# Reordering the quarter products of a seven-product FFN output and moving an epsilon from GpSimd to ScalarE (top-k attention and SwiGLU)

## The chip, the cores and the metric

The kernel runs on one core of one Trainium2 chip. The metric is the device time of one execution in microseconds (us); lower is better. The names of the engines in the profile are: PE is TensorE's matmuls, PEld its weight loads, DVE is VectorE, ACT is ScalarE, POOL is GpSimd, SP is SyncE, which here only issues transfers.

## The reference: what is computed

Attention over 8 batches and 8 heads with 576 positions of 64 elements, in which each query keeps only its 32 largest scores, and then a SwiGLU block on the 4608 rows of 512 that come out. All is float32.

```python
# attention: q, k, v of shape (8, 8, 576, 64)
scores = scale * np.matmul(q, k.transpose(0, 1, 3, 2))
kth = np.partition(scores, -top_k, axis=-1)[..., -top_k:-top_k + 1]   # top_k = 32
scores = np.where(scores >= kth, scores, -1000000000.0)
scores = scores - np.max(scores, axis=-1, keepdims=True)
attn = np.exp(scores)
attn = attn / (np.sum(attn, axis=-1, keepdims=True) + 1e-09)
x = np.matmul(attn, v)                      # brought to (4608, 512)
# FFN: w_gate, w_val of (512, 1536), w_out of (1536, 512)
g = x @ w_gate
silu = g * (1.0 / (1.0 + np.exp(-g)))
out = silu * (x @ w_val) @ w_out
```

## The kernel before

**Units.** The attention is cut into 160 units: one batch, one tile of 128 queries (the fifth tile of a batch has 64) and one pair of heads. In one pass of the main loop several units are in work at once, each at another step. VectorE picks the 32 largest scores of unit n, GpSimd and ScalarE form the exponentials of unit n-1, VectorE and ScalarE normalize unit n-2, TensorE transposes unit n-3 and multiplies unit n-4 with v. The order of instructions on every engine is fixed when the program is built: each engine takes its own in the order in which the code emits them.

**FFN.** As soon as 256 rows of the attention's result are there (`done`), their FFN can be computed: a block. There are 18 blocks, and `feed` is a generator that gives a block's matmuls in pieces. The main loop puts such pieces among the steps of the attention, as many as a credit allows.

**The epsilon, before.** `weigh` takes exp with the row sum as an accumulated output. A unit later, `normalize` first adds the epsilon on GpSimd, then takes the reciprocal on VectorE and scales on ScalarE:

```python
def penalize(n):
    ...
    nc.gpsimd.tensor_scalar_mul(bias[:, 0:nh], m[:, 0:nh, 0], -scale)
    nc.gpsimd.tensor_tensor(e[:, every], e[:, every], sc[:, every], ALU.add)      # L338

def weigh(n):
    ...
    for t, hs in enumerate(heads):
        nc.scalar.activation(                                                     # L347
            e[:, hs], e[:, hs], AF.Exp, bias=bias[:, t : t + 1], scale=scale,
            accum_out=tot[:, t : t + 1],
        )
    st["tot"] = tot

def normalize(n):
    ...
    nc.gpsimd.tensor_scalar_add(tot[:, 0:nh], tot[:, 0:nh], EPS)                  # L357
    yield
    nc.vector.reciprocal(tot[:, 0:nh], tot[:, 0:nh])                              # L359
    yield
    for t, hs in enumerate(heads):
        nc.scalar.mul(e[:, hs], e[:, hs], tot[:, t : t + 1])                      # L362
```

**The main loop**, cut to the order in which one pass emits its steps:

```python
flush(on_act)              # ScalarE work that the FFN pieces left for later
next(norm, None)           # GpSimd: epsilon of unit n-2
penalize(n - 1)            # GpSimd: bias, e + sc
flush(on_pool)             # GpSimd work that was left for later
run(turn(n - TURN))        # TensorE: transposes of e (L374), ScalarE: copies (L375)
finish_unit(n - VALUES)    # TensorE: e times v (L403)
next(nxt, None)            # TensorE: scores of unit n+1 (L281, L295)
weigh(n - 1)               # ScalarE: exp
run(nxt)                   # ScalarE: copies of these scores to sc (L286, L300)
dve(2, beside=False)       # VectorE: top-k steps of unit n
...
pieces(2)                  # FFN pieces on TensorE
flush(on_act)
flush(on_pool)
dve(1)
dve(1)
next(norm, None)           # VectorE: reciprocal
run(norm)                  # ScalarE: scaling
...                        # more top-k steps and up to 7 more pieces
```

**The seven products.** For the last matrix product of a block (all blocks but the first) the kernel uses a scheme with seven products in place of eight. The 256 rows are halved into early and late, the 1536 inner elements into two halves, the 512 outputs into two halves. P1 to P7 are called quarters here: six matmuls each (twelve records in the profile[...]) into one PSUM area. Their operands are sums and differences that GpSimd forms in place in `hs`, in `s32` (which takes the place of `xT`) and in the weights:

```python
def quarter(i, ps):
    for m in range(MQ):                       # MQ = 6
        s, r = m // 2, m % 2
        lhsT = {
            1: lambda: hs[s][:, r, early],
            2: lambda: hs[s + MS // 2][:, r, early],
            3: lambda: hs[s][:, r, late],
            4: lambda: hs[s + MS // 2][:, r, late],
            5: lambda: hs[s][:, r, late],
            6: lambda: s32[:, m],
            7: lambda: s32[:, m],
        }[i]()
        nc.tensor.matmul(ps, lhsT, T[i][m], start=m == 0, stop=m == MQ - 1)      # L543
        if m % 3 == 2:
            yield 0.75
...
# order: P1, P7, P5, P6, then
    def keep_y():
        nc.scalar.copy(b[:], y_ps[:])                                             # L577
        def sum_up():                         # tt is a GpSimd addition, L529
            tt(b[:, 1], b[:, 0], b[:, 1])
            tt(o[:, 1, DH:], o[:, 1, DH:], b[:, 1])
            tt(a[:], a[:], b[:, 1:2].to_broadcast([P, 2, DH]))
        on_pool.append(sum_up)

    yield from quarter(6, y_ps[:, 1])
    on_act.append(keep_y)
    flush(on_act)
    flush(on_pool)
    for s in range(MS // 2):                                                      # L591
        nc.gpsimd.tensor_tensor(
            hs[s][:, :, late],
            hs[s + MS // 2][:, :, early],
            s32[:, 2 * s : 2 * s + 2],
            ALU.subtract,
        )
    x_ps2 = ps_f.tile([P, 2, DH], FP32, tag="f", name="x_ps")
    yield from quarter(4, x_ps2[:, 1])
    yield from quarter(3, x_ps2[:, 0])
    ...
    def rest_x():
        nc.scalar.copy(middle, x_ps2[:])                                          # L605
        on_pool.append(lambda: tt(middle, middle, a[:]))
    on_act.append(rest_x)
    y_ps2 = ps_f.tile([P, DH], FP32, tag="f", name="y_ps")
    yield from quarter(2, y_ps2[:])
    def rest_y():
        nc.scalar.copy(o[:, 0, 0:DH], y_ps2[:])                                   # L613
        def stores():
            tt(o[:, 0, 0:DH], o[:, 0, 0:DH], b[:, 0])
            for t in range(2):
                store(o[:, t, :], kb * BLK + t * P)
        on_pool.append(stores)
    on_act.append(rest_y)
```

The pool `ps_f` has three PSUM buffers, which the FFN's tiles take in turn. `on_act` and `on_pool` are lists of work for ScalarE and GpSimd that is emitted at the next flush.

Of the kernel before, what the change touches and what calls it, by code (L numbers as in the profile page):

```python
# [8 lines left out]
AF = mybir.ActivationFunctionType  # L9
ALU = mybir.AluOpType  # L10
FP32 = mybir.dt.float32
# [4 lines left out]
P = 128  # L16
# [3 lines left out]
EPS = 1.0e-9  # L20
# [7 lines left out]
def kernel(  # L28
# [37 lines left out]
    nc = tc.nc  # L66
# [14 lines left out]
    consts = ctx.enter_context(tc.tile_pool(name="consts", bufs=1))  # L81
# [7 lines left out]
    ps_f = ctx.enter_context(tc.tile_pool(name="ps_f", bufs=3, space=PSUM))  # L89
# [5 lines left out]
    for i in range(NV):  # L95
        vt = consts.tile([P, P], FP32, name=f"vlast{i}")
        nc.vector.memset(vt[:], 0.0)
        vlast.append(vt)
    wg = consts.tile([P, KC, DFF], FP32, name="wg")
    wv = consts.tile([P, KC, DFF], FP32, name="wv")  # L100
    wo = consts.tile([P, MC, DM], FP32, name="wo")
# [86 lines left out]
    def rounding(n):  # L188
        for _ in range(n):
            next(weight, None)  # L190
# [70 lines left out]
    def n_heads(qt):  # L261

        return 1 if qt == J else 2
# [39 lines left out]
    def select(n):  # L303

        nh = n_heads(units[n][1])
        sc = state[n]["sc"]
        m = small.tile([P, 2, TOP_K], FP32, tag="m", name="m", bufs=2)
        heads = [slice(t * S, (t + 1) * S) for t in range(nh)]
        rest = work.tile([P, 2 * S], FP32, tag="rest", name="rest", bufs=1)
        e = work.tile([P, 2 * S], FP32, tag="e", name="e", bufs=4)  # L310
        state[n] |= dict(m=m, e=e, heads=heads)
        cur = sc
        rounds = TOP_K // 8
        for r in range(rounds):
            for t, hs in enumerate(heads):
                nc.vector.max(m[:, t, 8 * r : 8 * r + 8], cur[:, hs])  # L316
                yield
            if r < rounds - 1:
                for t, hs in enumerate(heads):
                    nc.vector.match_replace(  # L320
                        rest[:, hs], m[:, t, 8 * r : 8 * r + 8], cur[:, hs], LOWEST
                    )
                    yield
                cur = rest
        for t, hs in enumerate(heads):
            nc.vector.tensor_scalar(  # L326
                e[:, hs], sc[:, hs], m[:, t, TOP_K - 1 : TOP_K], FAR, ALU.is_lt, ALU.mult
            )
# [12 lines left out]
    def weigh(n):  # L341

        st = state[n]
        e, heads, bias = st["e"], st["heads"], st.pop("bias")
        tot = small.tile([P, 2], FP32, tag="tot", name="tot")
        for t, hs in enumerate(heads):
            nc.scalar.activation(  # L347
                e[:, hs], e[:, hs], AF.Exp, bias=bias[:, t : t + 1], scale=scale,
                accum_out=tot[:, t : t + 1],
            )  # L350
        st["tot"] = tot

    def normalize(n):
        st = state[n]
        tot, e, heads = st.pop("tot"), st["e"], st.pop("heads")
        nh = len(heads)
        nc.gpsimd.tensor_scalar_add(tot[:, 0:nh], tot[:, 0:nh], EPS)  # L357
        yield
        nc.vector.reciprocal(tot[:, 0:nh], tot[:, 0:nh])  # L359
        yield  # L360
        for t, hs in enumerate(heads):
            nc.scalar.mul(e[:, hs], e[:, hs], tot[:, t : t + 1])  # L362
# [62 lines left out]
    def store(o, g0):  # L425

        at = g0
        while at < g0 + P:
            b, c = divmod(at, S)
            j, p0 = divmod(c, P)  # L430
            n = min(g0 + P - at, S - c, P - p0)
            r0 = b * S + (c if j == J else J * p0 + j)
            dst = out[r0 : r0 + n, :] if j == J else out[r0 : r0 + J * (n - 1) + 1 : J, :]
            nc.sync.dma_start(dst, o[at - g0 : at - g0 + n, :])
            at += n

    on_act, on_pool = [], []

    def flush(queue):
        while queue:  # L440
            queue.pop(0)()

    def feed(kb):
# [50 lines left out]
        o = ffn.tile([P, 2, DM], FP32, tag="o", name="o", bufs=1)  # L494
# [29 lines left out]
        DH = DM // 2  # L524
        y_ps = ps_f.tile([P, 2, DH], FP32, tag="f", name="y_ps")
        x_ps = ps_f.tile([P, 2, DH], FP32, tag="f", name="x_ps")

        def tt(out, in0, in1):
            nc.gpsimd.tensor_tensor(out, in0, in1, ALU.add)  # L529

        def quarter(i, ps):
            for m in range(MQ):
# [10 lines that stand above are left out]
                nc.tensor.matmul(  # L543
                    ps, lhsT, T[i][m], start=m == 0, stop=m == MQ - 1
                )
                if m % 3 == 2:
                    yield 0.75
# [19 lines left out]
        a = ffn.tile([P, 2, DH], FP32, tag="gv", name="p57", bufs=3)  # L567
# [6 lines left out]
        b = ffn.tile([P, 2, DH], FP32, tag="gv", name="p16", bufs=3)  # L574
# [15 lines left out]
# [4 lines that stand above are left out]
                s32[:, 2 * s : 2 * s + 2],  # L594
                ALU.subtract,
            )
        x_ps2 = ps_f.tile([P, 2, DH], FP32, tag="f", name="x_ps")
        yield from quarter(4, x_ps2[:, 1])
        yield from quarter(3, x_ps2[:, 0])
        middle = o[:].rearrange("p t d -> p (t d)")[:, DH : 3 * DH].rearrange(  # L600
            "p (t d) -> p t d", t=2
        )

        def rest_x():
            nc.scalar.copy(middle, x_ps2[:])  # L605
            on_pool.append(lambda: tt(middle, middle, a[:]))

        on_act.append(rest_x)
        y_ps2 = ps_f.tile([P, DH], FP32, tag="f", name="y_ps")
        yield from quarter(2, y_ps2[:])  # L610

        def rest_y():
            nc.scalar.copy(o[:, 0, 0:DH], y_ps2[:])  # L613

            def stores():
                tt(o[:, 0, 0:DH], o[:, 0, 0:DH], b[:, 0])
                for t in range(2):
                    store(o[:, t, :], kb * BLK + t * P)

            on_pool.append(stores)  # L620

        on_act.append(rest_y)

    NU = len(units)
    todo = list(range(NBLK))
# [21 lines left out]
    def fetch(n):  # L647

        b, qt, hp = units[n]
        i = b * NHP + hp  # L650
        if qt == 0:
            yield from prep(i)
        if qt == J and i + NHP < len(pairs):
            load(i + NHP)

    def pieces(n):
        for _ in range(n):
            if credit[0] >= 1:
                credit[0] -= piece()

    def run(steps):
        for _ in steps:
            pass
# [18 lines left out]
    for n in range(NU + VALUES):  # L682
        nh = n_heads(units[n][1]) if n < NU else 1
        topk = select(n) if n < NU else no
        over[n - 1] = normalize(n - 1) if 0 <= n - 1 < NU else no
        nxt = scores(n + 1) if n + 1 < NU else no
        ahead = fetch(n + 2) if n + 2 < NU else no
        norm = over.pop(n - 2, no)

        def dve(k, beside=True):  # L690

            for _ in range(k * nh):
                next(topk, None)
                due[0] += 5 / 11 if beside else 0
                if due[0] >= 1:
                    due[0] -= 1
                    rounding(1)

        if n >= NU - NHP:
            credit[0] = 8.0  # L700
        else:
            credit[0] = min(credit[0] + (4.45 if nh == 2 else 2.25), 8.0)
        flush(on_act)
        next(norm, None)
        if 0 <= n - 1 < NU:
            penalize(n - 1)
        flush(on_pool)
        if 0 <= n - TURN < NU:
            run(turn(n - TURN))
        if n >= VALUES:  # L710
            finish_unit(n - VALUES)
        next(nxt, None)
        if 0 <= n - 1 < NU:
            weigh(n - 1)
        run(nxt)

        dve(2, beside=False)
        if 2 <= n + 2 < NHP:
            load(n + 2)
        if n < NHP:  # L720
            load_v(n)
        pieces(2)
# [4 lines that stand above are left out]
        next(norm, None)  # L727
        run(norm)
        next(ahead, None)
        pieces(1)  # L730
        next(ahead, None)
        dve(1)
        pieces(1)
        dve(2)
        run(topk)
        pieces(6)
# [50 lines left out]
```

## Time and profile before

| | |
|---|---|
| time, median of 3 runs (lowest to highest) | 1920.52 us (1919.66 to 1921.52) |
| span of the profiled execution | 1918.4 us |
| TensorE matmul busy | 1727.4 us, 90% |
| VectorE busy | 1621.0 us, 84% |
| ScalarE busy | 1170.2 us, 61% |
| GpSimd busy | 1062.6 us, 55% |
| mean granted TensorE clock | 0.952 of full speed |

A profile is read here in this way. The busy table gives one sum for each engine over the whole execution. The slices cut the execution into 40 equal parts, with one digit each for the busy tenths. The waits tell, for an instruction's line and the engine that it runs on, which instruction ended the idle time ahead of it: the total in us, how often, and the longest. In the timeline, each row is an instruction, or several of one kind that follow each other, with its start, its length and, in brackets, the idle time before it and what ended it. Lines such as L591 are lines of the kernel before. An engine's idle time costs something only where that engine, at that moment, sets how fast the rest can go on.

### The profile page before, as it was taken

The numbers are of one execution on the slowest core, as the hardware profiler recorded it, in microseconds if no ns is written. First come the engines' busy times: TensorE is split into PE (matmuls) and PEld (weight loads), VectorE is DVE, ScalarE is ACT, GpSimd is POOL, SyncE is SP. The second block draws the span as 40 slices with busy tenths as digits, with TensorE's granted clock in tenths as the row PEclk, the third lists the DMA queues.
The fourth block names the chain that finished last, engine by engine and source line by source line (L and its number), as shares of the span: only waits on it lengthen the run. The fifth ranks groups of instructions, "written<-read, shape, count | busy, mean of one in ns | idle before, by whom it ended". The sixth has DMA issues, their size and how long they took to land.

```text
span 1918.4 us, 30988 instructions
## 1 busy us (share of the span) xinstructions
PE 1727.4 (90%) x10756; PEld 1418.9 (74%) x10756; DVE 1621.0 (84%) x3476; ACT 1170.2 (61%) x2855; POOL 1062.6 (55%) x1167
## 2 busy tenths in 40 slices
PE   3437789989999999898999999989999999899988
PEld 2336558778888778786778877878788878787877
DVE  7999889998899979897889989988898979998300
ACT  5656666666666566566656666656675657565432
POOL 4556655645565646464455655645556645556534
PEclk7668899989999999899999999999999999999989
DMA  7322212000300011000210003000210002000000
GB/s 186 87 80 79 66 31 59 12 1 2 81 7 12 1 46 44 12 1 13 54 35 1 12 10 80 1 12 1 64 26 12 1 14 51 12 1 12 1 12 11
DMA packets 111261, 59.68 MB, mean 31 GB/s; under 512 B 89088, under 2 KB 97280, under 8 KB 111104
## 3 DMA queue, kind: packets, MB, share of 16 engines
q1 hardware_dynamic: 109904, 57.41, 11.3%
q8 instruction: 85, 1.39, 0.3%
q14 instruction: 72, 0.59, 0.1%
q10 hardware_dynamic: 1200, 0.30, 0.1%
HBM read 48.23 MB, written 9.44 MB: 30 GB/s over the span
## 4 chain that ended last, share of the span: by engine, by line
PE 70%; POOL 10%; DVE 8%; ACT 7%; issue 4%; DMA 0%; SPq 0%; POOLq 0%; ACTq 0%; DVEq 0%
PE f L457 35%; PE av L403 7%; PE etps L374 7%; PE x_ps L543 7%; PE s L295 5%; PE y_ps L543 4%; DVE m L316 4%; POOL e L338 4%; DVE rest L320 3%; ACT e L347 2%; ACT sc L300 2%; PE s L281 2%; POOL p L529 1%; PE av L394 1%; POOL size L124 1%
## 5 line engine op out<-in xcount | busy, mean ns | idle before, releaser
L316 DVE MAX8 m<-rest 128x8 f32<-128x576 f32 x864 | 614.5, 745 | 2.2
L320 DVE MATCH_REPLACE8 rest<-m,rest 128x576 f32<-128x576 f32 x576 | 423.6, 741 | 0.0
L457 PE MATMUL f<-xT,wg 128*128 128x256 f32 x1728 | 405.6, 385 | 0.0
L457 PE MATMUL f<-xT,wv 128*128 128x256 f32 x1728 | 397.9, 381 | 0.0
L338 POOL TENSOR_TENSOR e<-e,sc 128x1152 f32<-128x1152 f32 (+1 forms) x160 | 382.9, 2393 | 27.0 <-DVE e L326 26.8
L457 PEld LDWEIGHTS f<-xT,wg 128*128 128x128 f32 x1728 | 324.9, 191 | 66.7 <-issue 23.7
L457 PEld LDWEIGHTS f<-xT,wv 128*128 128x128 f32 x1728 | 324.3, 190 | 55.6 <-issue 13.5
L485 POOL TENSOR_TENSOR h<-h,half_g 128x512 f32<-128x512 f32 x108 | 138.4, 1282 | 366.2 <-ACT h L484 363.0
L374 PE MATMUL etps<-ident,e 128*128 128x128 f32 (+1 forms) x1312 | 191.2, 291 | 130.3 <-POOL size L114 46.8
L347 ACT ACTIVATE e<-e,bias 128x576 f32<-128x576 f32 x288 | 222.0, 776 | 125.6 <-POOL e L338 125.3
L374 PEld LDWEIGHTS etps<-ident,e 128*128 128x128 f32 (+1 forms) x1312 | 161.8, 149 | 162.7 <-POOL size L114 50.1
L375 ACT COPY et<-etps 128x512 f32<-128x512 f32 (+1 forms) x448 | 185.0, 483 | 144.6 <-PE etps L374 143.0
L316 DVE MAX8 m<-sc 128x8 f32<-128x576 f32 x288 | 205.2, 748 | 75.7 <-ACT sc L300 46.9
L490 POOL TENSOR_TENSOR h<-h,val 128x512 f32<-128x512 f32 x108 | 140.2, 1298 | 158.3 <-ACT val L489 158.2
L362 ACT ACTIVATE e<-e,tot 128x576 f32<-128x576 f32 x288 | 210.7, 782 | 5.4 <-DVE tot L359 5.1
L320 DVE MATCH_REPLACE8 rest<-m,sc 128x576 f32<-128x576 f32 x288 | 211.6, 741 | 0.0
L295 PE MATMUL s<-kqT 64*128 64x288 f32 x1024 | 173.0, 446 | 8.9 <-ACT kqT L255 6.0
L403 PE MATMUL av<-et,v 128*64 128x128 f32 (+1 forms) x2560 | 174.6, 282 | 0.0
L300 ACT COPY sc<-s 128x288 f32<-128x288 f32 x512 | 164.7, 408 | 2.5 <-PE s L295 2.5
L482 ACT ACTIVATE h<-f 128x512 f32<-128x512 f32 x108 | 64.8, 600 | 164.0 <-PE f L457 163.5
L326 DVE TENSOR_SCALAR e<-sc,m 128x576 f32<-128x576 f32 x288 | 159.0, 589 | 3.8 <-DVE m L316 0.5
L403 PEld LDWEIGHTS av<-et,v 128*64 128x64 f32 x2560 | 137.6, 146 | 23.4 <-issue 7.3
(70 smaller groups left out, 2035.0 us busy)
## 6 DMA issues: line engine op xcount, KB each, us to landing
kq_in<-in_k_dram SPq DMA_DIRECT2D x64, 128.0 KB, 2.8
v<-in_v_dram SPq DMA_DIRECT2D x32, 256.0 KB, 3.2
kq_in<-in_q_dram SPq DMA_DIRECT2D x62, 128.0 KB, 3.0
w<-in_moe_w_gate_dram SPq DMA_DIRECT2D x24, 256.0 KB, 2.7
w<-in_moe_w_val_dram SPq DMA_DIRECT2D x24, 256.0 KB, 2.7
w<-in_moe_w_out_dram SPq DMA_DIRECT2D x24, 256.0 KB, 2.6
out_dram<-o SPq DMA_DIRECT2D x40, 128.0 KB, 2.4
out_dram<-o SPq DMA_DIRECT2D x16, 256.0 KB, 2.4
```

The costliest lines, as they stand in the source:

```text
L295: nc.tensor.matmul(ps[:, 0:half], slab[d, q0 : q0 + P], slab[d, k0 : k0 + half])
L300: nc.scalar.copy(sc[:, i * half : (i + 1) * half], ps[:, 0:half])
L316: nc.vector.max(m[:, t, 8 * r : 8 * r + 8], cur[:, hs])
L320: nc.vector.match_replace(rest[:, hs], m[:, t, 8 * r : 8 * r + 8], cur[:, hs], LOWEST)
L338: nc.gpsimd.tensor_tensor(e[:, every], e[:, every], sc[:, every], ALU.add)
L347: nc.scalar.activation(e[:, hs], e[:, hs], AF.Exp, bias=bias[:, t : t + 1], scale=scale, accum_out=tot[:, t : t + 1],)
L362: nc.scalar.mul(e[:, hs], e[:, hs], tot[:, t : t + 1])
L374: nc.tensor.transpose(ps[0:kl, c * P : (c + 1) * P], e[:, k0 : k0 + kl], ident[:])
L375: nc.scalar.copy(et[0:kl, c0 : c0 + cn, :], ps[0:kl, 0 : cn * P].rearrange("p (c j) -> p c j", c=cn),)
L403: nc.tensor.matmul(av[hh * R : (hh + 1) * R, 0:ql], v_last[:, hh, :] if c == J else vt[:, hh, c, :], moving, start=last and c == 0, stop=c ...
L457: nc.tensor.matmul(ps[:, i, :], w[:, kc, m * P : (m + 1) * P], x[:, kc, :], start=(kc == 0), stop=(kc == KC - 1),)
L543: nc.tensor.matmul(ps, lhsT, T[i][m], start=m == 0, stop=m == MQ - 1)
```

## The change

Two things are changed.

- Of the last three quarters of a block, P2 now comes first and P4 and P3 follow. Before it was P4, P3, P2. P3 reads what the subtraction behind P6 (L591) writes, and P2 doesn't; the order is meant to give GpSimd more time for it. The copies and additions of the results change places accordingly: the quarter area of P2 is finished first, and the addition of the middle half of the output now stands ahead of the stores.
- The epsilon is added to the row sums by ScalarE, as an Identity activation with the epsilon as its bias, right behind exp. GpSimd no longer does it a unit later, so the reciprocal on VectorE doesn't depend on GpSimd's queue any more.

```diff
+    eps = consts.tile([P, 1], FP32, name="eps")
+    nc.vector.memset(eps[:], EPS)
...
                 accum_out=tot[:, t : t + 1],
             )
+        nh = len(heads)
+        nc.scalar.activation(tot[:, 0:nh], tot[:, 0:nh], AF.Identity, bias=eps[:])
         st["tot"] = tot

     def normalize(n):
...
-        nc.gpsimd.tensor_scalar_add(tot[:, 0:nh], tot[:, 0:nh], EPS)
-        yield
         nc.vector.reciprocal(tot[:, 0:nh], tot[:, 0:nh])
...
+        y_ps2 = ps_f.tile([P, DH], FP32, tag="f", name="y_ps")
+        yield from quarter(2, y_ps2[:])
+
+        def rest_y():
+            nc.scalar.copy(o[:, 0, 0:DH], y_ps2[:])
+            on_pool.append(lambda: tt(o[:, 0, 0:DH], o[:, 0, 0:DH], b[:, 0]))
+
+        on_act.append(rest_y)
         x_ps2 = ps_f.tile([P, 2, DH], FP32, tag="f", name="x_ps")
         yield from quarter(4, x_ps2[:, 1])
         yield from quarter(3, x_ps2[:, 0])
...
         def rest_x():
             nc.scalar.copy(middle, x_ps2[:])
-            on_pool.append(lambda: tt(middle, middle, a[:]))
-
-        on_act.append(rest_x)
-        y_ps2 = ps_f.tile([P, DH], FP32, tag="f", name="y_ps")
-        yield from quarter(2, y_ps2[:])
-
-        def rest_y():
-            nc.scalar.copy(o[:, 0, 0:DH], y_ps2[:])

             def stores():
-                tt(o[:, 0, 0:DH], o[:, 0, 0:DH], b[:, 0])
+                tt(middle, middle, a[:])
                 for t in range(2):
                     store(o[:, t, :], kb * BLK + t * P)

             on_pool.append(stores)

-        on_act.append(rest_y)
+        on_act.append(rest_x)
...
         flush(on_act)
-        next(norm, None)
         if 0 <= n - 1 < NU:
             penalize(n - 1)
```

## The prediction

> **What bounds the kernel now.** I read the page first: the busy table and the slices.
>
> ```profile
> PE 1727.4 (90%) x10756; PEld 1418.9 (74%) x10756; DVE 1621.0 (84%) x3476; ACT 1170.2 (61%) x2855; POOL 1062.6 (55%) x1167
> ...
> PE   3437789989999999898999999989999999899988
> ...
> PEclk7668899989999999899999999999999999999989
> ```
>
> TensorE is busiest, VectorE follows, and the granted clock is below full speed mainly in the first slices. An average over different stages says little, so I asked for three stages (columns: stage, length, busy time of PE, PEld, DVE, ACT, POOL, then clock, DMA share, GB/s):
>
> ```profile
> 0.00:340.00 340.00, 223.10 (x1255) 169.80 (x1256) 301.85 (x689) 208.55 (x532) 197.76 (x260) 0.80 0.30 83
> 340.00:1850.00 1510.00, 1442.52 (x9228) 1195.76 (x9227) 1319.15 (x2788) 946.35 (x2295) 836.05 (x878) 0.98 0.08 20
> 1850.00:1919.00 69.00, 61.82 (x276) 53.38 (x275) 0.00 (x0) 15.27 (x28) 28.77 (x30) 0.97 0.04 8
> ```
>
> Up to about 340 us VectorE and the chain around it set the pace (302 of 340 us). After that TensorE does (1443 of 1510, then 62 of 69), so what is left to win there is its idle time, about 1579 - 1504 = 75 us. The waits of TensorE from 340 us to the end name it (total us, times, longest):
>
> ```profile
> PE x_ps L543 <- POOL h L591: 29.7, 13, 3.2
> PE etps L374 <- issue: 27.0, 15, 3.8
> PE etps L374 <- ACT e L362: 11.7, 9, 4.1
> ```
>
> The largest is P3 waiting for the difference that GpSimd writes into `hs` at L591. The other two are transposes that wait for the scaled `e`, at places where little FFN work is left to fill TensorE. One instance of the first, from the timeline (start, length, engine, line, operation, idle before it):
>
> ```profile
> 762.76 2.75 PE L543 MATMUL x_ps<-t,h 128*128 128x256 f32 x12
> ...
> 764.09 0.60 ACT L577 COPY p<-y_ps 128x512 f32<-128x512 f32 x1
> 764.77 0.73 POOL L529 TENSOR_TENSOR p<-p 128x256 f32<-128x256 f32 x1 [1.04 <-ACT p L577]
> ...
> 765.58 0.72 POOL L529 TENSOR_TENSOR o<-o,p 128x256 f32<-128x256 f32 x1
> 766.26 1.27 POOL L529 TENSOR_TENSOR p<-p,p 128x512 f32<-128x512 f32 x1
> ...
> 767.49 2.11 POOL L591 TENSOR_TENSOR h<-h,xT 128x256 f32<-128x256 f32 x3
> ...
> 768.27 4.54 PE L543 MATMUL x_ps<-wo,h 128*128 128x256 f32 x12 [2.75 <-POOL h L591]
> ```
>
> `x_ps<-t,h` is P4; its next twelve, `x_ps<-wo,h`, are P3. Behind P6, ScalarE copies its sums (L577), GpSimd makes three additions of results (L529) and only then the operands for P3 (L591). P4 covers part of that, 2.6 us; then TensorE stands for 2.75 us. P2 needs nothing of it (it reads the early columns of `hs`), yet comes after P3.
>
> The epsilon shows in two views: the waits of VectorE from 340 to 1850 us, and the instructions that touch `tot`.
>
> ```profile
> DVE tot L359 <- POOL tot L357: 104.0, 41, 12.5
> DVE m L316 <- ACT sc L300: 41.1, 34, 4.9
> ```
>
> ```profile
> L357 POOL TENSOR_SCALAR tot<-tot x160: 214/219/892, 39.5 to 1841.0; 128x2 f32<-128x2 f32 x128, 128x1 f32<-128x1 f32 x32
> ```
>
> VectorE loses 104 us to an operation of 0.22 us that stands in GpSimd's queue behind the FFN products. But nearly all of it falls where TensorE is the bound, so it is mostly slack of an engine that isn't the limit.
>
> [...] exp, tanh, absolute values and scalings alternate all through, with one ACT_TABLE_LOAD (1.28 us) at the very start. [...] after the waits at 765, 977 and 1257 us P3 took 4.54, 4.54 and 4.45 us instead of 2.75 to 2.86, after the ten others it did not.
>
> **The change, part by part.**
>
> (a) *P2 first.* Same quarter products, same number; by the instruction order P2 takes P4's place, P4 that of P3 and P3 that of P2, and the attention work between them stays where it is. So P3's operands get the length of one more quarter, 2.6 us. Thirteen waits sum to 29.7 us; five are longer than 2.6 (2.75, 3.18, 3.07, 2.75, 3.19) and leave together 1.9. Saving: 27.8 us, on TensorE's own path.
>
> (b) *Clock.* Without those gaps the three slow P3 come back to 2.8: 3 x 1.7 = 5 us saved.
>
> (c) *Given back.* Where the FFN runs dry after a block, VectorE becomes the bound. A saving passes through only as far as VectorE was itself idle there. At 768 the saving is 2.75 + 1.7, VectorE's idle time ahead of the dry stretch is 0.34 + 2.89; at 1647 it is 2.75 against 0.32 + 1.20. About 1.2 each: 2.4 us lost.
>
> (d) *Epsilon.* GpSimd loses 160 x 0.22 us; with its start, 0.30 us from one operation to the next (780.12 to 780.42 in the timeline), ahead of the `bias` and `e` + `sc` operations. ScalarE gains 160 Identities behind exp and ahead of the copies of the scores. Each must wait until the accumulator readout behind exp (median 188 ns) has ended; up to now the next copy overlapped it. [...] Where the chain runs GpSimd, exp, scores, VectorE, a unit pays +0.4 - 0.3 = 0.1. That is the early stage: 20 of the 160 units start their addition before 290 us, so +2 us. In the TensorE-bound units it is hidden on both sides. About six block ends go dry (381, 779, 883, 1270, 1656, 1760 us); there the Identity delays the scores by 0.4, and the last copy of the block is now the larger one (L605, 0.59 us, instead of L613, about 0.4): 6 x 0.6 = 3.6 us. In the last units one addition of 0.7 us leaves GpSimd's chain. Sum: +4.9 us.
>
> (e) *End.* After the last quarter the copy is 0.59 instead of 0.37 us and the addition 1.27 instead of 0.72: +0.8 us.
>
> (f) *VectorE's reciprocal* no longer waits. Its 104 us become waits for `sc` from ScalarE, which TensorE releases: zero for the end.
>
> Sum: -27.8 - 5 + 2.4 + 4.9 + 0.8 = -24.7 us, so 1920.5 - 24.7 = 1896 us.
>
> **Rivals.**
>
> *VectorE was the real limit, and the epsilon wait is what matters.* For it: 104 us of waits, 84% busy, units of about 9 us in dry stretches against 10.5 in full ones. Against it: in full stretches the matmuls follow each other without a gap for 10.5 us a unit, and the longest reciprocal waits (8.9, 10.0, 12.6 us near 1800) lie where TensorE has no gap at all. If true, 50 us or more would go: below 1870.
>
> *ScalarE's added step sits on the path.* For it: exp and the score copies are on the chain of waits in the early and dry stretches, and ScalarE works in order. Against it: 61% busy, and 2 us between the scaled `e` and the transposes in full units. If the 0.4 us counted in half of the 160 units, 32 us would eat the gain: about 1923.
>
> *A new wait in place of the old one.* P4 now writes the PSUM tile that the copy of P6's sums (L577) has to leave first. At 763 that copy ends at 764.69, 1.9 us after P6, and P4 will not come before 2.6: tight, not late. If each block lost 0.5 us so, 8 us less gain: about 1904.
>
> *The gap only moves.* A full TensorE would meet attention work sooner and wait longer for `e` at L374 (38.7 us now). Against it: in most blocks the dry stretch starts with VectorE waiting 2 to 3 us for scores. At worst half of (a) is lost: about 1910.
>
> **Range and chances.** Part (a) is well fixed, since wait and cover are both measured; it carries the direction. (c) and (d) are guesses good to some 6 us each, and the clock can add or take 5. I give 1885 to 1909. Faster by over 2% would need less than 1882, which asks for the first rival in part: 0.08. Slower by over 2% would need the second and the last together and more: 0.02.
>
> **What would show it right or wrong.** In the profile after: (a) the wait of `x_ps` for the L591 difference falls from 29.7 to under 4 us; (b) no P3 above 3 us for twelve; (c) and (d) TensorE's waits at the transposes stay within 35 to 48 us, the first 340 us within 4 us; [...] (f) reciprocal waits near zero and waits for `sc` grown by some 60 to 100 us. I am wrong if the new wait appears at P4 behind the L577 copy, if the early stage changes by over 8 us, or if TensorE's idle time falls by 28 us while the span does not.

## The result and the profile after

The changed kernel takes 1892.8 us (median of 4 runs, 1889.0 to 1895.5) against 1920.1 us before: 0.986 of the time, 95% interval 0.984 to 0.988, so 27 us less. The forecast was 1896, with a range of 1885 to 1909. The sum was right, but the quarter order was worth more than forecast and the epsilon cost more, and that the two errors nearly cancelled was luck, as the experiments show.

The busy table and the granted clock of the changed kernel:

```profile
PE 1723.2 (91%) x10756; PEld 1419.1 (75%) x10756; DVE 1632.0 (86%) x3477; ACT 1212.3 (64%) x3015; POOL 1023.2 (54%) x1007
...
PEclk7668899989999999899999999999999999999989
```

ScalarE has 160 instructions more and 42 us more work, GpSimd 160 fewer and 39 us less. TensorE does the same work. Its waits from 330 us to the end (total us, times, longest); the change adds two lines to the file, so L593 is what L591 was, L376 what L374 was, L364 what L362 was:

```profile
PE etps L376 <- issue: 22.1, 12, 3.0
PE etps L376 <- ACT e L364: 16.3, 9, 2.1
PE x_ps L545 <- POOL h L593: 2.7, 3, 0.9
```

P3's wait fell from 29.7 to 2.7 us; the waits at the transposes stayed at 38.4 (38.7 before). The waits of VectorE over the whole execution, first before, then in the changed kernel:

```profile
DVE tot L359 <- POOL tot L357: 105.7, 42, 12.5
DVE m L316 <- ACT sc L300: 46.9, 37, 4.9
...
DVE m L316 <- ACT sc L286: 28.4, 22, 3.9
```

```profile
DVE m L318 <- ACT sc L288: 70.9, 24, 11.0
DVE m L318 <- ACT sc L302: 55.4, 41, 4.2
...
DVE tot L361 <- ACT tot L354: 15.6, 2, 11.6
```

The reciprocal's waits for GpSimd (105.7 us over the whole execution) are gone. In their place VectorE waits 126 us for the scores, where it had waited 75, and twice for the Identity among the last units.

### The profile page after: what moved, and what is told of

The parts are those of the page before. It is cut to its first block, busy times and chain, and to the rows that moved or that the text cites. A ratio compares the mean times of both kernels' runs of the same rounds, so it can differ in the third digit from the quotient of the medians.

```text
span 1892.5 us, 30875 instructions
## 1 busy us (share of the span) xinstructions
PE 1723.2 (91%) x10756; PEld 1419.1 (75%) x10756; DVE 1632.0 (86%) x3477; ACT 1212.3 (64%) x3015; POOL 1023.2 (54%) x1007
## 3 DMA queue, kind: packets, MB, share of 16 engines
q1 hardware_dynamic: 109904, 57.41, 11.6%
## 4 chain that ended last, share of the span: by engine, by line
PE 79%; ACT 7%; POOL 7%; DVE 4%; issue 2%; DMA 0%; SPq 0%; POOLq 0%; ACTq 0%
PE f L459 38%; PE av L405 8%; PE x_ps L545 8%; PE etps L376 8%; PE s L297 6%; PE y_ps L545 5%; POOL e L340 3%; ACT e L349 2%; PE s L283 2%; ACT sc L302 2%; PE av L396 1%; DVE m L318 1%; DVE rest L322 1%; PE kqps L252 1%; PE o_ps L505 1%
## 5 line engine op out<-in xcount | busy, mean ns | idle before, releaser
L376 PE MATMUL etps<-ident,e 128*128 128x128 f32 (+1 forms) x1312 | 191.0, 291 | 132.2 <-POOL size L116 48.1
L376 PEld LDWEIGHTS etps<-ident,e 128*128 128x128 f32 (+1 forms) x1312 | 161.9, 150 | 163.9 <-POOL size L116 51.3
L364 ACT ACTIVATE e<-e,tot 128x576 f32<-128x576 f32 x288 | 211.5, 787 | 5.3 <-DVE tot L361 5.1
L328 DVE TENSOR_SCALAR e<-sc,m 128x576 f32<-128x576 f32 x288 | 173.4, 639 | 3.4
```

Source lines behind the costliest of these rows:

```text
L376: nc.tensor.transpose(ps[0:kl, c * P : (c + 1) * P], e[:, k0 : k0 + kl], ident[:])
```

## The experiments

Each kernel was timed in five rounds beside the kernel before on the same chip, whose medians were 1919.5 to 1920.2 us. Ratios are to that kernel.

### Each part alone

P2 first, the epsilon on GpSimd as before (against the changed kernel, cut):

```diff
-        nc.scalar.activation(tot[:, 0:nh], tot[:, 0:nh], AF.Identity, bias=eps[:])
+        nc.gpsimd.tensor_scalar_add(tot[:, 0:nh], tot[:, 0:nh], EPS)   # in normalize, a unit later
```

> Only the quarter order is changed; GpSimd still adds the epsilon a unit later. Theory A (the gain is P3's wait, filled by P2): nearly the whole gain is here, 24 to 30 us under the kernel before, so 1890 to 1896, and P3's wait for the subtraction falls from 29.7 to under 4 us. Theory B (the gain comes from VectorE no longer waiting for the epsilon): at most 8 us, about 1912 or more. Theory C (the Identity on ScalarE costs on the path): clearly faster than the changed kernel, by 8 us or more, 1885 or less.

Measured: 1881.2 us, ratio 0.9795 (0.9782 to 0.9809). So the order alone brings 38 us, more than both parts together. P3's wait is gone as theory A had it, but the time lies beyond A's 24 to 30 us and in the range of theory C. Its waits of TensorE from 330 us on (lines as in the kernel before):

```profile
PE etps L374 <- issue: 22.5, 12, 3.7
PE etps L374 <- ACT e L362: 16.0, 9, 2.1
PE x_ps L543 <- POOL h L591: 1.7, 3, 0.6
```

With some small ones TensorE's waits in that stretch are 42.3 us, where they were 69.0: 27 of the 37 us by which the span fell. The rest is in the busy time. One stage row from 330 us to the end, first of the kernel before, then of this one (length, then busy PE, PEld, DVE, ACT, POOL, clock, DMA):

```profile
330.00:1919.00 1589.00, 1514.35 (x9558) 1257.50 (x9554) 1329.15 (x2811) 968.29 (x2339) 869.87 (x913) 0.98 0.08 20
```

```profile
330.00:1919.00 1589.00, 1502.34 (x9552) 1252.16 (x9548) 1328.11 (x2809) 967.68 (x2338) 869.87 (x913) 0.99 0.08 20
```

The matmuls took 12 us less (over the whole execution, with 10756 records in both, 1727.4 and 1715.7 us). The granted clock goes with it. In the traces of the kernel before and of the changed one it is either full or half, for stretches of 3.41 us or whole multiples (the last one ends with the trace). From 330 us to the last matmul it was half for 51 us before and for 31 us here. A P3 in a stretch at half clock took 4.54 us instead of 2.86, the 1.7 us that half of 3.4 us is, so 20 us less are worth up to 10.

The reverse, the epsilon moved and the quarters left as P4, P3, P2 (against the kernel before, cut):

```diff
-        nc.gpsimd.tensor_scalar_add(tot[:, 0:nh], tot[:, 0:nh], EPS)
+        nc.scalar.activation(tot[:, 0:nh], tot[:, 0:nh], AF.Identity, bias=eps[:])   # in weigh
```

> Only the epsilon is moved to ScalarE; the quarters stay P4, P3, P2. Theory A: no gain, 0 to 6 us slower than the kernel before (1920 to 1926), though the reciprocal's 104 us of waits for GpSimd are gone, with waits for the scores in their place. Theory B: 15 us or more faster, below 1905. Theory C: 8 us or more slower, 1928 or more.

Measured: 1929.9 us, ratio 1.0055 (1.0043 to 1.0068), 10 us slower. Theory B is out: VectorE's waits for GpSimd had gone here too, and nothing was won. P3's wait was a little longer than before:

```profile
PE x_ps L545 <- POOL h L593: 31.9, 13, 3.5
```

The cost is also above theory A's 0 to 6 us and lies in the range of theory C.

### The epsilon left out

P2 first and no addition of the epsilon at all:

```diff
-        nc.scalar.activation(tot[:, 0:nh], tot[:, 0:nh], AF.Identity, bias=eps[:])
```

> P2 first, and the epsilon left out altogether: neither GpSimd nor ScalarE adds it (in float32 a sum of at least 1 does not change by 1e-9). Theory A: the early stage, 0.3 us a unit shorter on GpSimd and 0.4 on ScalarE against the changed kernel, gains 5 to 9 us on the changed kernel: about 1885 to 1888. Theory C: 12 us or more on the changed kernel, since the Identity also counts in the later stages: below 1881. Theory B: like the changed kernel, within 3 us.

And the kernel before without it:

```diff
-        nc.gpsimd.tensor_scalar_add(tot[:, 0:nh], tot[:, 0:nh], EPS)
-        yield
```

> The kernel before without any addition of the epsilon (left out; float32 sums of at least 1 do not change by 1e-9). VectorE's reciprocal waits for nobody on GpSimd, and ScalarE has no added work. Theory A: 4 to 8 us faster than before, from the early stage alone: 1912 to 1916. Theory B: 20 us or more faster, below 1900, since this is the wait removed at no cost. Theory C expects the same as A here and tells itself apart by the distance to the kernel with the epsilon moved: over 12 us against 5 to 9.

Measured: 1877.3 us (0.9784, 0.9770 to 0.9797) and 1914.3 us (0.9972, 0.9963 to 0.9982). Both kernels leave the epsilon out. The distance to the kernels that have it gives its price in each place. On GpSimd: 1881.2 - 1877.3 = 3.9, or 1919.5 - 1914.3 = 5.2 us. On ScalarE behind exp: 1892.8 - 1877.3 = 15.5, or 1929.9 - 1914.3 = 15.6 us. The move costs 10 to 12 us net, as theory C had it and not theory A. Leaving the addition out, which also frees VectorE from GpSimd, is worth 5 us, not the 20 or more of theory B.

### Where ScalarE does it, and how often

The Identity made twice behind exp:

```diff
         nc.scalar.activation(tot[:, 0:nh], tot[:, 0:nh], AF.Identity, bias=eps[:])
+        nc.scalar.activation(tot[:, 0:nh], tot[:, 0:nh], AF.Identity, bias=eps[:])
```

> The changed kernel with the Identity on ScalarE made twice behind exp (the epsilon is added twice, which float32 sums of at least 1 do not show). Theory C, the Identity costs because it stands ahead of the score copies: another 8 to 16 us, 1901 to 1909. Theory A as predicted (about 0.1 us for each of 20 units and 0.4 for six block ends, now 0.4 for all 26): another 10 us is the most, 1899 to 1903, two thirds of it before 340 us. If the cost of the single one was chance of the clock: within 4 us of the changed kernel.

Measured: 1906.4 us, ratio 0.9935 (0.9923 to 0.9948), 13.6 us over the changed kernel. That is in theory C's range and beyond theory A's. The price is no accident of one kernel: the second step costs about what the first did. Half of it fell into the early stage: the addition of `e` and `sc` in unit 24 began at 340.6 us in the changed kernel and at 348.0 here.

The single Identity, but behind the copies of the scores:

```diff
+    def add_eps(n):
+        tot, nh = state[n]["tot"], len(state[n]["heads"])
+        nc.scalar.activation(tot[:, 0:nh], tot[:, 0:nh], AF.Identity, bias=eps[:])
 ...
             weigh(n - 1)          # without the Identity
         run(nxt)
+        if 0 <= n - 1 < NU:
+            add_eps(n - 1)
```

> The changed kernel, but ScalarE makes the Identity behind the copies of the scores, not between exp and these copies. The same work on ScalarE, off the chain to VectorE. Theory C: most of the Identity's cost goes, 8 to 14 us under the changed kernel, near 1880, close to the kernel with no epsilon at all (1877). If it is the work of ScalarE itself that costs, not its place: within 4 us of the changed kernel.

Measured: 1886.8 us, ratio 0.9825 (0.9811 to 0.9838). Its place is worth 6 us of the 15.5. That falls short of the 8 to 14 expected by theory C and is more than the 4 of the other; 9.5 us remain for the same work further back in ScalarE's queue, and I have not separated them. The timeline of ScalarE in the changed kernel shows the step itself:

```profile
115.12 0.19 ACT L349 ACTIVATION_READ_ACCUMULATOR e<-e,bias 128x1 f32 x1
115.34 0.29 ACT L354 ACTIVATE tot<-tot,eps 128x2 f32<-128x2 f32 x1
115.54 0.68 ACT L302 COPY sc<-s 128x288 f32<-128x288 f32 x2
```

The readout behind exp ends at 115.31, the Identity starts then, and the score copies 0.2 us later. From the start of the first exp (113.68) to the copies it is 1.86 us; in the kernel before, 112.70 to 114.23, 1.53. So the step adds 0.33 us; its length was not the mistake.

### P3's wait removed or filled in other ways

The kernel before, in its own order, with the subtraction for P3 ahead of the three additions of results:

```diff
         on_act.append(keep_y)
         flush(on_act)
-        flush(on_pool)
         for s in range(MS // 2):
             nc.gpsimd.tensor_tensor(hs[s][:, :, late], ..., ALU.subtract)
+        flush(on_pool)
```

> The kernel before, with its order P4, P3, P2 and its epsilon, but GpSimd makes the subtraction for P3 ahead of the three additions of results behind P6, not after them. P3's wait is removed in another way than by P2. If the gain of the order is only this wait and the clock that it costs, this comes near to P2 first alone: 30 to 38 us under the kernel before, 1882 to 1890, with TensorE's busy time down by 8 to 12 us as there. If P2's place did something else, the gain stays under 25 us although the wait is gone.

Measured: 1881.6 us, ratio 0.9805 (0.9792 to 0.9819). The same 38 us by another road, with no wait of P3 for L591 left: removing the wait is enough, whatever the place of P2. From 330 us on TensorE's busy time fell by 11.6 us (1514.35 to 1502.71), as with P2 first, and half clock from 51 to 34 us.

The kernel before with P4 computed twice, so that TensorE is busy where it waited:

```diff
         yield from quarter(4, x_ps2[:, 1])
+        for _ in quarter(4, x_ps2[:, 1]):
+            pass
```

> The kernel before with P4 computed twice (the second overwrites the first): TensorE is busy for 2.6 us where it waited for P3's operands. Without any effect of idle time on the clock: 17 x 2.6 = 44 us more work less 28 us of waits filled, so 16 us over the kernel before, about 1936. If the waits cost clock, as supposed from the fall of TensorE's busy time by 12 us with P2 first, 8 to 13 us of it come back: 1923 to 1928.

Measured: 1927.8 us, ratio 1.0043 (1.0030 to 1.0055). P3's wait and TensorE's stage from 330 us on:

```profile
PE x_ps L543 <- POOL h L591: 2.0, 5, 0.6
```

```profile
330.00:1926.00 1596.00, 1549.96 (x9762) 1293.12 (x9758) 1326.41 (x2811) 970.20 (x2339) 869.49 (x913) 0.99 0.08 20
```

The added work is 17 x 2.6 = 44.2 us, and 27.7 us of P3's waits were filled. Of the 16.5 us that this gives, only 7.7 were lost; 8.8 came back, as the second forecast had it. It shows in the busy time, which grew by 35.6 us instead of 44.2, and in the clock: half for 38 us, where it was 51. Idle time was replaced by work and nothing else was changed, so idle time cost clock, beyond itself.

Both ways together, once without and once with the epsilon (on GpSimd):

```diff
         flush(on_act)
-        flush(on_pool)
         for s in range(MS // 2): ...              # the subtraction for P3
+        flush(on_pool)
+        yield from quarter(2, y_ps2[:])
         yield from quarter(4, x_ps2[:, 1])
         yield from quarter(3, x_ps2[:, 0])
-        yield from quarter(2, y_ps2[:])
```

> P2 first, the epsilon left out (float32 sums of at least 1 do not show it), and the subtraction for P3 ahead of the three additions. With P2 first only 1.7 us of P3's wait are left, so the earlier subtraction should add next to nothing to the kernel with P2 first and no epsilon: 1873 to 1880. If the two ways of removing P3's wait each bring something else than the wait, they add up: below 1868.

> P2 first, epsilon on GpSimd as before, and the subtraction ahead of the three additions. The epsilon is kept, so this computes all that the reference does. The wait explains the gain: like P2 first alone, 1877 to 1884. If both orders count for themselves: below 1870.

Measured: 1872.6 us (0.9752, 0.9739 to 0.9765), without the epsilon, and 1874.0 us (0.9761, 0.9747 to 0.9774), with everything that the reference computes. Both lie between the two forecasts: 0.4 and 3 us under the range of the wait alone, 5 and 4 us above what two separate gains would give. The earlier subtraction thus added 4.7 and 7.2 us, though only 1.7 us of P3's wait were left, so the wait is not all of its gain. In the second kernel the waits at the transposes are 35.4 us against 38.5 with P2 first alone, busy time from 330 us on is 1499.1 against 1502.3, and half clock 20 us against 31; why these waits shrank is open. It is the best kernel here that keeps the epsilon: 2.4% under the kernel before.

### The epsilon on VectorE

P2 first, the addition right ahead of the reciprocal:

```diff
+        nc.vector.tensor_scalar_add(tot[:, 0:nh], tot[:, 0:nh], EPS)
         nc.vector.reciprocal(tot[:, 0:nh], tot[:, 0:nh])
```

> P2 first, the epsilon added on VectorE right ahead of the reciprocal, so neither GpSimd's nor ScalarE's chain has it. VectorE's added work is about 0.2 us a unit (the reciprocal of the same size takes 0.15). If only chains count, the cost is that of about 26 units in which VectorE sets the pace: 3 to 7 us over the kernel with P2 first and no epsilon, so 1880 to 1884. If 160 x 0.2 us count in full: about 1909.

Measured: 1894.2 us, ratio 0.9865 (0.9852 to 0.9879), 17 us over the kernel without epsilon: neither forecast. The groups of VectorE show why (count, busy us, mean ns, idle before):

```profile
L357 DVE TENSOR_SCALAR tot<-tot 128x2 f32<-128x2 f32 (+1 forms) x160 | 69.9, 437 | 15.3 <-ACT e L347 15.3
L358 DVE RECIPROCAL tot<-tot 128x2 f32<-128x2 f32 (+1 forms) x160 | 26.5, 166 | 5.5
```

An addition of two elements takes 437 ns in the mean (median 160), the reciprocal of the same two 166. In the timeline, one of the long ones beside GpSimd's work:

```profile
667.46 2.61 POOL L338 TENSOR_TENSOR e<-e,sc 128x1152 f32<-128x1152 f32 x1
668.05 2.05 DVE L357 TENSOR_SCALAR tot<-tot 128x2 f32<-128x2 f32 x1
```

It began at 668.05 and ended with the other, at 670.1. So did all 56 additions that took over 0.3 us: each ended within 0.06 us of the end of a GpSimd TENSOR_TENSOR. That could lie in the form of the instruction or in its place behind GpSimd's work. To tell the two apart, the sum and the epsilon were put side by side and added by a reduction, a form with one input of pairs (against the kernel above, cut):

```diff
-        nc.vector.tensor_scalar_add(tot[:, 0:nh], tot[:, 0:nh], EPS)
+        nc.vector.tensor_reduce(inv[:, 0:nh], tot[:, 0:nh, :], axis=X, op=ALU.add)   # pairs (sum, EPS)
```

> As with the epsilon on VectorE, but added by a reduction over pairs (sum, epsilon) instead of a scalar addition. The scalar additions of [128 x 2] took 0.44 us in the mean, up to 2.22, and the 56 long ones ended with an addition of GpSimd. [...] the reductions stay near 0.16 to 0.2 us with none above 0.4, and the kernel comes within 3 to 7 us of the one without epsilon: 1880 to 1885. If VectorE's small operations get long for another reason (their place behind GpSimd's work, whatever their form), the reductions are as long and the time stays near 1894.

Measured: 1882.6 us, ratio 0.9808 (0.9795 to 0.9821), 5.3 us over the kernel without epsilon. The reductions, minimum, median and maximum in ns:

```profile
L363 DVE TENSOR_REDUCE inv<-sums x160: 136/146/156, 45.2 to 1805.3; 128x2 f32<-128x4 f32 x128, 128x1 f32<-128x2 f32 x32
```

None is long, in the same place of the same queue, though 97 of the 160 lay wholly inside a GpSimd operation. So it was the form of the instruction that made it wait for GpSimd (up to 2222 ns against at most 156), and not its place. Why GpSimd's work holds up one form and not the other is not shown.

## Why the prediction was right, point by point

**The bound and the cause** were right. TensorE's wait for P3's operands, with the clock that it cost, was nearly all of the gain of the order, and VectorE's 104 us were slack: the first rival is refuted by the epsilon alone (10 us slower) and by leaving the epsilon out (5 us).

**(a) P2 first**: 27.8 us of waits forecast; 28.0 went with P2 first alone, 27.0 in the changed kernel.

**(b) Clock**: right in kind, too small. I counted three slow P3 (5 us); that the waits ahead of them had brought the clock down was my estimate. Two of these stretches before (stage, length, PE, PEld, DVE, ACT, POOL, clock):

```profile
765.00:775.00 10.00, 7.25 (x44) 5.70 (x42) 9.66 (x22) 1.24 (x3) 7.54 (x9) 0.83 0.00 0
...
1256.00:1266.00 10.00, 7.59 (x46) 5.93 (x46) 7.61 (x17) 1.49 (x6) 7.21 (x9) 0.83 0.01 2
```

and the same work with P2 first alone:

```profile
758.00:768.00 10.00, 8.74 (x59) 6.96 (x57) 9.27 (x21) 4.67 (x15) 8.68 (x12) 1.00 0.00 0
...
1236.00:1246.00 10.00, 9.29 (x62) 7.44 (x60) 7.58 (x17) 4.47 (x14) 8.62 (x12) 1.00 0.01 2
```

The clock is back at full there, as forecast. But before, half clock also followed 16 to 18 us after some of the waiting P3, at the end of their blocks (768, 1259 and 1647 us), and part of that went too: 9 to 12 us of busy time in the three kernels without P3's wait (12.0, 11.6, 8.6), 7 to 10 by the clock alone. For the quarter order the term should have been that. In the changed kernel hardly any of it arrived: half clock from 330 us on is 48 us, against 51 before and 31 with P2 first alone. One block end before, in the changed kernel and with P2 first alone:

```profile
765.00:800.00 35.00, 28.23 (x165) 22.44 (x164) 31.78 (x68) 19.32 (x50) 17.04 (x18) 0.85 0.04 16
```

```profile
765.00:800.00 35.00, 30.03 (x172) 24.71 (x171) 33.46 (x75) 22.09 (x56) 14.81 (x13) 0.85 0.04 16
```

```profile
765.00:800.00 35.00, 30.25 (x189) 25.03 (x188) 34.60 (x73) 24.43 (x61) 17.08 (x16) 0.95 0.04 16
```

**(c) Given back**: 2.4 us forecast; not settled. With P2 first alone, the addition of `e` and `sc` began 7.5 us earlier than before in unit 64 and 12.8 us earlier in unit 67: 5.2 us won at the block of 768 us, where wait and slow P3 together were 4.4. At 1647 us it was 3.4 (27.0 to 30.4) for a wait of 2.75. But behind each of these waits half clock also fell from 6.8 to 3.4 us, worth up to 1.7, so up to 6.1 and 4.5 us could have come. About 1 us is missing at each, near the 1.2 forecast, but less than the 1.7 us that one stretch of 3.4 us at half clock costs; nothing here shows whether VectorE took it.

**(d) Epsilon**: +4.9 forecast, +10 to +12 measured. The 0.4 us a unit was an estimate of mine that no trace of the kernel before shows. The step that failed is where these 0.4 us count: "In the TensorE-bound units it is hidden on both sides", with 0.6 us at each of six block ends. The length was right: the Identity takes 294 to 298 ns, begins 32 or 33 ns behind the end of the readout in all 160 units, and the chain grew by 0.33 us in the one shown above. Before, the operation behind a readout began 92 to 148 ns ahead of its end. The Identity brought no table load: the changed kernel has one ACT_TABLE_LOAD, as before. Unit 24 began 1.8 us later than before in the changed kernel, near my +2, though 4.0 with the epsilon alone, whose early code is the same; this stage scatters by 2 us. The rest, 6 to 10 us, came later, where I had 2.9. What stands there is mostly clock: from 330 us on, half clock for 48 us against 31 with P2 first alone, and 61 with the epsilon alone against 51 before. That is worth up to 8.5 and 5 us; my terms had no clock for the Identity. TensorE's busy time over the whole execution agrees (1723.2 against 1715.7, 1734.7 against 1727.4), with the waits from 330 us on nearly equal (43.1 and 42.3 for the first pair). How the 0.33 us on ScalarE bring half clock to the block ends is not shown.

**(e) End**: +0.8 forecast. From the end of the last matmul to the end it is 7.1 us instead of 5.0, so +2.1. The term lacked the stores: before, the first of the four stores of the last block went out at 1912.95, ahead of the last addition; now all four wait for the addition of the middle half.

**(f)** The waits of the reciprocal became waits for the scores, as forecast, by 51 us and not 60 to 100.

The second rival (ScalarE's step on the path) was half true: 15.5 us of the 32 that it allowed. No wait of P4 for the PSUM copy appeared, and the gap did not move elsewhere.

Sum of the order's terms, (a), (b), (c) and (e): -29.6 forecast, -38.4 measured. Of (d): +4.9 and about +11. The mechanism of the order was right; the total was right by luck, because it was 9 us too careful in the one and 6 us too careless in the other.

## What to carry to other kernels

Where TensorE was the bound here, a gap in it cost more than its length: 27 us of gaps cost another 7 to 12 in clock, so the first look goes to a fixed order in which something that is ready stands behind something that waits. The price of a small operation was not its length but where it stood and what it waited for: 160 additions of an epsilon cost 4 to 5 us on GpSimd, 15.5 on ScalarE behind exp and 17 or 5 on VectorE, by the form of the instruction. Two changes that come together are worth measuring apart: here one half gave 38 us and the other took 11 of them back.

## What the runs showed of the hardware that I had not expected

VectorE's scalar form of addition on two elements took up to 2.2 us, to the end of a GpSimd operation in flight (56 of 160 took over 0.3 us; nine more lay inside one and were short), while the reciprocal of the same size (0.17 us in the mean there, and at most 0.17 in the kernel before, where 79 of 160 lay wholly inside a GpSimd operation) and the reduction (at most 0.16 us) did not. The same shows in the masks of the top-k, a scalar form of 576 elements, first in the kernel before, then in the changed one:

```profile
L326 DVE TENSOR_SCALAR e<-sc,m 128x576 f32<-128x576 f32 x288 | 159.0, 589 | 3.8 <-DVE m L316 0.5
```

```profile
L328 DVE TENSOR_SCALAR e<-sc,m 128x576 f32<-128x576 f32 x288 | 173.4, 639 | 3.4
```

Of these 288 masks, 39 before and 52 in the changed kernel took over 0.7 us, and a GpSimd operation ended inside each of them, 0.31 to 0.32 us ahead of the mask's own end. They took 14 us more once the reciprocal no longer waited for GpSimd; with P2 first alone, where it still does, they took 158.8. It is not what makes the Identity expensive: with P2 first and the epsilon left out they are as long, and that kernel is 15.5 us faster than the changed one:

```profile
L326 DVE TENSOR_SCALAR e<-sc,m 128x576 f32<-128x576 f32 x288 | 176.3, 648 | 3.8 <-DVE m L316 0.5
```

The clock changed only at multiples of 3.41 us from its last change, in the trace before as in the one after. Cut into intervals of that length, the stretch from 300 us to the last matmul shows when. Before, the clock fell from full to half 9 times, each time after an interval in which TensorE was busy for 0.16 to 1.10 us; after the other 448 intervals at full clock, all busy for 1.56 us or more, it stayed. In the changed kernel it fell 10 times, after 0.51 to 1.79 us of work, and stayed after 439 intervals, one of them with 1.52 us of work and the others with 1.99 or more. Each of the 19 times that it came back, TensorE had been busy for 2.99 us or more of the interval before. That fits the three slow P3 among thirteen waits before: those at 765, 977 and 1257 us left 0.66, 0.34 and 1.10 us of work in one interval, the ten others 1.56 us or more in each that they lay in. A wait of 3.18 us at 869 us lay across two intervals with 1.73 and 1.91 us of work and cost no clock; one of 2.41 us at 1257 us did. By what rule the clock is granted is not shown.
